# Retention attention in front of a feed-forward block: four 64x64 tiles of TensorE, two sequences loaded head by head, the state summed in SBUF

## Chip, cores and metric

One core of one Trainium2 chip. The metric is the device time of one execution in microseconds (us); lower is better. The kernel before takes 219.63 us (median of four runs, 219.4 to 220.01; the prediction was made from the first three, median 219.77). Engines: PE is TensorE's matmul, PEld its weight load, DVE is VectorE, ACT is ScalarE, POOL is GpSimd, SP the queue that issues stores and transposes.

## The reference

A decayed linear attention over 4 sequences of 768 positions with 8 heads of 64, then a feed-forward block with a sine activation. Its output is 3072 x 512 in float32.

```python
# q, k, v: (4, 8, 768, 64)
for t in range(S):
    state = gamma * state + outer(k[t], v[t])        # 64 x 64 per head
    y[t] = (1 / sqrt(64)) * q[t] @ state
x = y as (3072, 512)
h = x @ w_in                                         # (3072, 2048)
s = sin(alpha * h)
out = (h + s * s / (alpha + 1e-9)) @ w_out           # (3072, 512)
```

## The kernel before

Each sequence is cut into six chunks of 128 positions, so there are 24 chunks, taken in the order "first chunk of each sequence, then the rest of sequence 0, 1, 2, 3". The decay is divided out beforehand, so that the state becomes a plain running sum. Per chunk there are four kinds of small matmul, together called a burst here: scores (k against q), old state times q, masked scores times v (the mix), and the sum of k times v that is added to the state.

```python
def stage_S(j):                    # the state's sum lives in PSUM over the whole sequence
    if c == 0:
        st["ps"] = psum.tile([128, NP, D], F32, name="ps", tag="ps")
    ...matmul(ps[64 * e:64 * e + 64, p, :], k of the head, v of the head,
              start=(c == 0 and p == 0), ...)
def keep_S(j, ps):                 # two copies of 64x256 on ScalarE, straight from PSUM
    nc.scalar.copy(s_bd[(j % NCH + 1) % 2][r, :, r], ps[r, :, :])
def stage_M(j):
    py = psum.tile([128, NP, 128], F32, name="py", tag="ty")
    ...old state, mix...
    ps = stage_S(j)
    nc.vector.tensor_mul(x, py, qg[:, c])            # xT
    keep_S(j, ps)
```

The feed-forward work is cut into slots. A slot is one 128-wide block of hidden units: four products into a PSUM tile `ph`, then sine and square on ScalarE, then on VectorE the sum `gT`, which also frees `ph`. Output matmuls into `po` fill TensorE between slots.

```python
class Slot:
    self.ph = psum.tile([128, nf, w], F32, name="ph", tag=tag, bufs=4 if tag == "mm" else 1)
    ...4 matmuls; nc.scalar.activation(out=self.s, in_=self.ph, func=Sin)
    def sq(self, eng):  # "A": Square on ScalarE, "D": s * s on VectorE
    def add(self):      # VectorE: gT = s * rec_alpha + ph
def ff_out(g, ts, f):
    if (g, ts) not in po:
        po[g, ts] = psum.tile([128, d_model], F32, name="po", tag="mm", bufs=4)
```

Count the PSUM in units of one 128x512 float32 tile. The scores tile `pa` has two units, `ps` one, `ty` one, the ring `mm` four: eight. While the first four chunks pass through the feed-forward block, two output accumulators are held open for some 20 us. `ps` and `ty` are free at that time, and the schedule puts them there:

```python
    po[0, 0] = psum.tile([128, d_model], F32, name="po", tag="ps")
    po[0, 1] = psum.tile([128, d_model], F32, name="po", tag="ty")
    F((0,), range(4))              # output matmuls that fill TensorE between slots
```

Of the kernel before, what the change touches and what calls it, by code (L numbers as in the profile page):

```python
# [15 lines left out]
def kernel(  # L16
# [9 lines left out]
):  # L26

# [45 lines left out]
    def load_chunk(j, names="qkv"):  # L73
        for name, src in (("q", q), ("k", k), ("v", v)):
            if name not in names:
                continue
            if name == "v":
                t = big.tile([128, H, D], BF16, name="vr", tag="vr", bufs=NJ)
            else:
                if ("qk", j) not in raw:  # L80
                    raw["qk", j] = big.tile([128, 2, H, D], BF16, name="qkr", tag="qkr", bufs=NJ)
                t = raw["qk", j][:, "qk".index(name)]
            nc.gpsimd.dma_start(out=t, in_=chunk_of(src, j))  # L83
            raw[name, j] = t

# [4 lines left out]
    def load_w_in(i):  # L90
        nc.gpsimd.dma_start(out=w_in[:, :, i * fw:(i + 1) * fw], in_=w_in_v[:, :, i * fw:(i + 1) * fw])
# [6 lines left out]
    for name, src in (("q", q), ("k", k)):  # L98
        near[name] = big.tile([128, H, D], F32, name=f"{name}0")
        nc.sync.dma_start(out=near[name], in_=chunk_of(src, 0))  # L100
        raw[name, 0] = big.tile([128, H, D], BF16, name=f"{name}b")
# [9 lines left out]
    def scale_v(j, eng):  # L111
        eng.tensor_mul(raw["v", j], raw["v", j], kg[:, j % NCH, :, None].to_broadcast([128, H, D]))  # L112
# [38 lines left out]
    for p in range(NP):  # L151
        for e in range(2):
            nc.vector.memset(lgp[64 * e:64 * e + 64, p:p + 1], lng[2 * p + e])
# [3 lines left out]
                         lg[:, None, :].to_broadcast([128, NCH, H]))  # L157
    qg = consts.tile([128, NCH, NP, C], F32, name="qg")
# [12 lines left out]
    s_bd = [big.tile([128, NP, 128], BF16, name=f"s_bd{i}") for i in range(2)]  # L171
# [3 lines left out]
    xT = {}  # L175

    def half_T(j, i, eng):
# [4 lines left out]
        for p in range(NP):  # L182
            nc.tensor.transpose(pt[:, p, :], raw["qk"[i], j][:, 2 * p:2 * p + 2, :].rearrange("p h d -> p (h d)"), ident)
# [6 lines left out]
    def stage_T(j, eng=None, tag="ty"):  # L190
        pt = psum.tile([128, 2 * NP, 128], BF16, name="pt", tag=tag, bufs=4 if tag == "mm" else 1)
        st["qkT", j] = work.tile([128, 2 * NP, 128], BF16, name="qkT", tag="qkT", bufs=6)
        for i in range(2):
            for p in range(NP):
                nc.tensor.transpose(pt[:, i * NP + p, :],
                                    raw["qk"[i], j][:, 2 * p:2 * p + 2, :].rearrange("p h d -> p (h d)"), ident)
# [5 lines left out]
    def turn(j):  # L202

        st["qkT", j] = work.tile([128, 2 * NP, 128], BF16, name="qkT", tag="qkT", bufs=6)
        nc.sync.dma_start_transpose(out=st["qkT", j], in_=raw["qk", j].rearrange("p i h d -> p (i h d)"))

    def stage_A(j):
        qkT = st["qkT", j]
        pa = psum.tile([128, 2, NP, 128], F32, name="pa", tag="pa")
        for p in range(NP):  # L210
            for e in range(2):
                r = slice(64 * e, 64 * e + 64)
                nc.tensor.matmul(pa[:, e, p, :], qkT[r, NP + p, :], qkT[r, p, :],  # L213
                                 start=(p == 0), stop=True, skip_group_check=True)
        aT = work.tile([128, 2, NP, 128], BF16, name="aT", tag="aT", bufs=2)
        m = dec.rearrange("p e n t -> p (e n) t") if j % NCH == 0 else mask_bc
        nc.vector.tensor_mul(aT.rearrange("p e n t -> p (e n) t"), pa.rearrange("p e n t -> p (e n) t"), m)  # L217
        st["aT", j] = aT

    def stage_S(j):  # L220
        c = j % NCH
        if c == 0:
            st["ps"] = psum.tile([128, NP, D], F32, name="ps", tag="ps")
        ps = st["ps"]
        for p in range(NP):
            for e in range(2):
                nc.tensor.matmul(ps[64 * e:64 * e + 64, p, :], raw["k", j][:, 2 * p + e, :], raw["v", j][:, 2 * p + e, :],  # L227
                                 start=(c == 0 and p == 0), stop=True, skip_group_check=True)
        return ps

    def keep_S(j, ps):
        for e in range(2):
            r = slice(64 * e, 64 * e + 64)
            nc.scalar.copy(s_bd[(j % NCH + 1) % 2][r, :, r], ps[r, :, :])  # L234

    def stage_M(j):
        c = j % NCH
# [3 lines left out]
        qkT, aT, vs = st["qkT", j], st["aT", j], raw["v", j]  # L241
        py = psum.tile([128, NP, 128], F32, name="py", tag="ty")
        if c > 0:
            for p in range(NP):
                for e in range(2):
                    r = slice(64 * e, 64 * e + 64)
                    nc.tensor.matmul(py[r, p, :], s_bd[c % 2][:, p, r], qkT[:, p, :],  # L247
                                     start=(p == 0), stop=True, skip_group_check=True)
        for p in range(NP):
            for e in range(2):  # L250
                nc.tensor.matmul(py[64 * e:64 * e + 64, p, :], vs[:, 2 * p + e, :], aT[:, e, p, :],  # L251
                                 start=(c == 0 and p == 0), stop=True, skip_group_check=True)
        x = xT[g][:, :, i * C:(i + 1) * C]
        if c == 0:
            nc.scalar.copy(x, py)
            return
        ps = stage_S(j) if c < NCH - 1 else None
        nc.vector.tensor_mul(x, py, qg[:, c])  # L258
        if ps is not None:
            keep_S(j, ps)  # L260
# [4 lines left out]
    class Slot:  # L265


        def __init__(self, g, f, cols=None, nf=1, tag="mm"):
# [7 lines left out]
            self.s = work.tile([128, nf, w], F32, name="s", tag="s", bufs=5)  # L276
            for m, f in enumerate(self.fs):
                for i in range(KS):
                    nc.tensor.matmul(self.ph[:, m, :], w_in[:, i, f * 128:(f + 1) * 128], xT[g][:, i, self.lo:self.hi],  # L279
                                     start=(m == 0 and i == 0), stop=(i == KS - 1), skip_group_check=True)  # L280
# [18 lines left out]
    end = (NG - 1, sizes[-1] - 1)  # L299

    def ff_out(g, ts, f):
# [4 lines left out]
        if f == FF - 1:  # L306
            take(g, ts)

    def take(g, ts):
        o_sb = work.tile([128, d_model], F32, name="o_sb", tag="o_sb", bufs=3)  # L310
        if (g, ts) == end:
            h = d_model // 2
            nc.vector.tensor_copy(o_sb[:, :h], po[g, ts][:, :h])
            nc.scalar.copy(o_sb[:, h:], po[g, ts][:, h:])
        else:
            nc.scalar.copy(o_sb, po[g, ts])  # L316
        nc.sync.dma_start(out=out_view[:, groups[g][ts], :], in_=o_sb)
# [5 lines left out]
    pal = psum.tile([128, FF], F32, name="pal", tag="ps")  # L323
# [22 lines left out]
    stage_A(e0)  # L346
# [3 lines left out]
    half_T(e1, 1, nc.vector)  # L350
    nc.tensor.transpose(pal, alpha_row, ident_f)
    stage_M(e0)
    grow(1)
    idle_work(1)
    stage_A(e1)
# [5 lines left out]
    stage_M(e1)  # L361
    grow(3)
    nc.scalar.copy(alpha_sb, pal)
    nc.scalar.activation(out=tiny, in_=warm[:, 0:1], func=ACTF.Sin)
    stage_A(e2)
# [4 lines left out]
    stage_M(e2)  # L370
# [22 lines left out]
    def A(j):  # L393
        return lambda: stage_A(j)

    def M(j):
        return lambda: stage_M(j)

    def SK(j):
        return lambda: keep_S(j, stage_S(j))  # L400
# [16 lines left out]
    for t in s_bd:  # L417
        nc.vector.memset(t, 0.0)
    b = early(1)
    a.sq("A").add()  # L420
    a = early(2)
    b.sq("A")
    c = early(3)
    a.sq("A")
    stage_T(e3)
    b.add()
    b = early(4, "ps")
    c.sq("A")
# [3 lines left out]
    stage_A(e3)  # L432
    c.add()
    c = early(6)
    a.sq("A")
    b.add()
    b = early(7)
    c.sq("A")
    stage_M(e3)
# [3 lines left out]
    po[0, 0] = psum.tile([128, d_model], F32, name="po", tag="ps")  # L443
    po[0, 1] = psum.tile([128, d_model], F32, name="po", tag="ty")
# [6 lines left out]
    a = Slot(0, 8)  # L451
    b = Slot(0, 4, (n3, n4), 4)
    a.sq("A").add()
    a = Slot(0, 9)
    b.sq("D").add()
    F((0, 1), (4,))
    b = Slot(0, 10)
    a.sq("A").add()
    F((0, 1), (5,))
    a = Slot(0, 11)  # L460
    b.sq("D").add()
    decay_table(4)
    F((0, 1), (6, 7))
    b = Slot(0, 12)
    a.sq("A").add()
    decay_table(5)
    F((0, 1), (8,))
    a = Slot(0, 13)
# [96 lines left out]
```

## Time and profile before

| | before |
|---|---|
| time, median of four | 219.63 us |
| span of the profiled run | 217.5 us |
| TensorE busy | 203.8 us, 94% |
| ScalarE, VectorE, GpSimd busy | 162.8, 128.1, 90.1 us |
| mean granted TensorE clock | 0.999 |

I cut the span into four stages at marks: the first product; the first 256-column product (the stage of chunks 5 and 6); the next 512-column stage (chunks 7 to 10); and the first output group of the 512-column stage after that. Rows of busy time by stretch give the stretch, its length, then busy us (and instructions) of PE, PEld, DVE, ACT and POOL, the granted clock, the share of the transfer engines and GB/s.

### The profile page before, as it was taken

The numbers are of one execution on the slowest core, as the hardware profiler recorded it, in microseconds if no ns is written. First come the engines' busy times: TensorE is split into PE (matmuls) and PEld (weight loads), VectorE is DVE, ScalarE is ACT, GpSimd is POOL, SyncE is SP. The second block draws the span as 40 slices with busy tenths as digits, with TensorE's granted clock in tenths as the row PEclk, the third lists the DMA queues.
The fourth block names the chain that finished last, engine by engine and source line by source line (L and its number), as shares of the span: only waits on it lengthen the run. The fifth ranks groups of instructions, "written<-read, shape, count | busy, mean of one in ns | idle before, by whom it ended". The sixth has DMA issues, their size and how long they took to land.

```text
span 217.5 us, 4218 instructions
## 1 busy us (share of the span) xinstructions
PE 203.8 (94%) x1634; PEld 107.5 (49%) x1661; DVE 128.1 (59%) x213; ACT 162.8 (75%) x311; POOL 90.1 (41%) x105
## 2 busy tenths in 40 slices
PE   7798899999989999999999999999999999999992
PEld 3444554467764545445455445454544544555540
DVE  4686659867895767766466566366464555233310
ACT  7678796658889999789768768777868876766610
POOL 8975335999889885896981000000000000000000
PEclk9999999999999999999999999999999999999999
DMA  9999999999999999999999146237011101111121
GB/s 132 151 193 191 205 207 164 154 207 161 164 151 182 163 120 154 112 160 175 135 188 107 23 96 77 60 60 96 7 47 51 48 0 51 48 48 48 51 94 50
DMA packets 99508, 24.67 MB, mean 113 GB/s; under 512 B 92304, under 2 KB 96416, under 8 KB 99488
## 3 DMA queue, kind: packets, MB, share of 16 engines
q0 software_dynamic: 77024, 13.37, 84.0%
q1 hardware_dynamic: 22464, 11.02, 26.4%
q8 instruction: 13, 0.21, 0.4%
q14 instruction: 7, 0.06, 0.1%
HBM read 27.27 MB, written 6.29 MB: 154 GB/s over the span
## 4 chain that ended last, share of the span: by engine, by line
PE 74%; DVE 9%; DMA 4%; POOL 4%; ACT 4%; issue 3%; POOLq 0%; ACTq 0%
PE po L304 35%; PE ph L279 31%; DMA qkr<-in_k_dram 4%; DVE gT L294 4%; PE py L247 3%; PE pa L213 2%; POOL qkr L83 2%; ACT s L282 2%; DVE aT L217 2%; PE py L251 2%; POOL vr L83 1%; DVE xT L258 1%; PE ps L227 1%; DVE s L289 1%; ACT s L287 1%
## 5 line engine op out<-in xcount | busy, mean ns | idle before, releaser
L294 DVE SCALAR_TENSOR_TENSOR gT<-s,rec_alpha,ph 128x512 bf16<-128x512 f32 (+3 forms) x120 | 74.1, 637 | 68.1 <-ACT s L287 67.5
L279 PE MATMUL ph<-xT,w_in 128*128 128x512 bf16 (+3 forms) x478 | 97.9, 336 | 1.1 <-DVE gT L294 0.6
L304 PE MATMUL po<-w_out,gT 128*128 128x512 bf16 x360 | 94.1, 379 | 3.8 <-issue 2.9
L282 ACT ACTIVATE s<-ph,alpha_sb 128x512 f32<-128x512 f32 (+3 forms) x120 | 69.6, 601 | 34.0 <-PE ph L279 33.9
L279 PEld LDWEIGHTS <-w_in 128*128 128x128 bf16 x480 | 45.5, 98 | 42.6 <-issue 2.1
L287 ACT ACTIVATE s<-s 128x512 f32<-128x512 f32 (+1 forms) x94 | 58.4, 621 | 2.6
L304 PEld LDWEIGHTS <-gT 128*128 128x128 bf16 x384 | 35.2, 98 | 38.2 <-issue 0.6
L112 POOL TENSOR_TENSOR vr<-vr,kg 128x512 bf16<-128x512 bf16 x21 | 22.0, 1056 | 12.2 <-DMA vr<-in_v_dram 12.2
L217 DVE TENSOR_TENSOR aT<-pa,mask 128x1024 bf16<-128x1024 f32 x20 | 24.4, 1220 | 0.3 <-PE pa L213 0.3
L83 POOL DMA_DIRECT2D vr<-in_v_dram x24 | 21.7, 904 | 3.0 <-DMA w_in<-in_moe_w_in_dram 1.7
L83 POOL DMA_DIRECT2D qkr<-in_q_dram x23 | 21.3, 925 | 4.0 <-DMA w_out<-in_moe_w_out_dram 1.6
L83 POOL DMA_DIRECT2D qkr<-in_k_dram x23 | 20.4, 887 | 3.8 <-DMA w_out<-in_moe_w_out_dram 3.3
L234 ACT CAST s_bd<-ps 64x256 bf16<-64x256 f32 x40 | 14.4, 360 | 2.4 <-PE ps L227 2.1
L316 ACT COPY o_sb<-po 128x512 f32<-128x512 f32 x23 | 13.1, 576 | 3.9 <-PE po L304 3.9
L258 DVE TENSOR_TENSOR xT<-py,qg 128x512 bf16<-128x512 f32 x20 | 13.7, 684 | 2.6 <-PE py L251 2.5
L328 PE MATMUL spare<-warm 128*128 128x512 bf16 x27 | 9.3, 465 | 1.4 <-DVE warm L131 1.2
L213 PEld LDWEIGHTS <-qkT 64*128 64x128 bf16 x192 | 5.4, 94 | 9.3 <-issue 7.1
L251 PE MATMUL py<-aT,vr 128*64 128x128 bf16 x192 | 9.5, 220 | 0.4 <-DVE rec_alpha L366 0.2
L213 PE MATMUL pa<-qkT 64*128 64x128 bf16 x192 | 9.5, 219 | 0.4 <-ACT qkT L186 0.2
L247 PE MATMUL py<-qkT,s_bd 128*64 128x128 bf16 x160 | 8.3, 224 | 0.7 <-DVE xT L258 0.7
L247 PEld LDWEIGHTS <-s_bd 128*64 128x64 bf16 x160 | 5.4, 109 | 4.8 <-issue 2.0
L251 PEld LDWEIGHTS <-vr 128*64 128x64 bf16 x192 | 6.9, 110 | 1.3 <-issue 1.0
(59 smaller groups left out, 68.8 us busy)
## 6 DMA issues: line engine op xcount, KB each, us to landing
out_dram<-o_sb SPq DMA_DIRECT2D x24, 256.0 KB, 2.3
vr<-in_v_dram POOLq DMA_DIRECT2D x24, 128.0 KB, 6.2
qkr<-in_q_dram POOLq DMA_DIRECT2D x23, 128.0 KB, 5.6
qkr<-in_k_dram POOLq DMA_DIRECT2D x23, 128.0 KB, 5.8
w_in<-in_moe_w_in_dram POOLq DMA_DIRECT2D x4, 512.0 KB, 11.1
w_out<-in_moe_w_out_dram POOLq DMA_DIRECT2D x4, 512.0 KB, 14.8
q<-in_q_dram SPq DMA_DIRECT2D x1, 256.0 KB, 3.4
k<-in_k_dram SPq DMA_DIRECT2D x1, 256.0 KB, 4.7
```

What stands on the lines that cost most here:

```text
L83: nc.gpsimd.dma_start(out=t, in_=chunk_of(src, j))
L112: eng.tensor_mul(raw["v", j], raw["v", j], kg[:, j % NCH, :, None].to_broadcast([128, H, D]))
L213: nc.tensor.matmul(pa[:, e, p, :], qkT[r, NP + p, :], qkT[r, p, :], start=(p == 0), stop=True, skip_group_check=True)
L217: nc.vector.tensor_mul(aT.rearrange("p e n t -> p (e n) t"), pa.rearrange("p e n t -> p (e n) t"), m)
L247: nc.tensor.matmul(py[r, p, :], s_bd[c % 2][:, p, r], qkT[:, p, :], start=(p == 0), stop=True, skip_group_check=True)
L251: nc.tensor.matmul(py[64 * e:64 * e + 64, p, :], vs[:, 2 * p + e, :], aT[:, e, p, :], start=(c == 0 and p == 0), stop=True, skip_group_che ...
L258: nc.vector.tensor_mul(x, py, qg[:, c])
L279: nc.tensor.matmul(self.ph[:, m, :], w_in[:, i, f * 128:(f + 1) * 128], xT[g][:, i, self.lo:self.hi], start=(m == 0 and i == 0), stop=(i = ...
L282: nc.scalar.activation(out=self.s[:, m, :], in_=self.ph[:, m, :], func=ACTF.Sin, scale=alpha_sb[:, f:f + 1])
L287: nc.scalar.activation(out=self.s, in_=self.s, func=ACTF.Square)
L294: nc.vector.scalar_tensor_tensor(gT[self.g][:, f, self.lo:self.hi], self.s[:, m, :], rec_alpha[:, f:f + 1], self.ph[:, m, :], op0=ALU.mult ...
L304: nc.tensor.matmul(po[g, ts], gT[g][:, f, ts * C:(ts + 1) * C], w_out[:, f, :], start=(f == 0), stop=(f == FF - 1))
```

## The change

The intent is to spend less TensorE time on attention, by three means, and a little at the end:

- Small matmuls are cut into 64x64 pieces, so that four of them lie on TensorE at once: old state and scores for sequences 0 and 1, scores, mix and sums for sequences 2 and 3. (Mix and sums of 0 and 1 keep their 128x64 tiles; the old state of 2 and 3 becomes four full 128x128 matmuls.)
- Sequences 2 and 3 are loaded head by head with 64 positions on each half of the partitions (`load_seq`), so that the block of scores that the mask makes zero is never computed (768 columns in place of 1024).
- The state is summed on VectorE in SBUF (`s_f`); the product of one chunk no longer lives in PSUM.
- The last output tile is stored in pieces of 256, 128 and 128 columns.

The diff, cut to its core:

```diff
-    def stage_S(j):
-        if c == 0:
-            st["ps"] = psum.tile([128, NP, D], F32, name="ps", tag="ps")
-    def keep_S(j, ps):
-            nc.scalar.copy(s_bd[(j % NCH + 1) % 2][r, :, r], ps[r, :, :])
+    def new_py(j):
+        st["py", j] = psum.tile([128, 2, 512], F32, name="py", tag="py")   # state sums in here too
+    def keep(j, py):
+        new = py[:, :, 256:384].rearrange("p b (m d) -> p m b d", m=2)
+        nc.vector.tensor_add(s_f, s_f, new)          # tensor_copy at the first chunk
+        nc.scalar.copy(s[half(0), :, 0:4:3], s_f[half(0)])
+        nc.scalar.copy(s[half(1), :, 1:3], s_f[half(1)])
+    def mix(j, first=None):
+        ...sums(now, py)
+        nc.vector.tensor_mul(x_of(j), py[:, :, 0:256]..., qg[:, c]...)
+        keep(now, py)
+    def burst(old, new, first=None):
+        inter(old)        # old state
+        scores(new)       # scores of the next chunk, and VectorE's masked product aT
+        mix(old, first)
...
-    po[0, 0] = psum.tile([128, d_model], F32, name="po", tag="ps")
-    po[0, 1] = psum.tile([128, d_model], F32, name="po", tag="ty")
...
-    a = Slot(0, 8)
+    a = Slot(0, 8, nf=2, tag="py")
...
-    a = Slot(0, 11)
-    b.sq("D").add()
+    b = Slot(0, 11)
+    a.sq("D").add()
     decay_table(4)
...
+    load_seq(2)
+    load_seq(3)
...
+    last_tile(NG - 1, sizes[-1] - 1)
```

`py` now has two units, and `ps` and `ty` are gone: pa 2, py 2, mm 4, again eight. Two pairs of slots of the first stage (8 and 9, 12 and 13) take `py` instead, and some squares move from ScalarE to VectorE. VectorE also scales 19 of the v tiles, in place of 3 (GpSimd did the others), and the slots around the fourth first chunk come in another order.

## The prediction

> **What bounds the kernel now.** I read the page first (busy shares, then the chain that ended last), then the TensorE timeline of one burst of attention, then the busy time by stage, then the GpSimd timeline, which shows when loads land. From the page:
>
> ```profile
> PE 203.8 (94%) x1634; PEld 107.5 (49%) x1661; DVE 128.1 (59%) x213; ACT 162.8 (75%) x311; POOL 90.1 (41%) x105
> ...
> DMA  9999999999999999999999146237011101111121
> ...
> PE 74%; DVE 9%; DMA 4%; POOL 4%; ACT 4%; issue 3%; POOLq 0%; ACTq 0%
> PE po L304 35%; PE ph L279 31%; DMA qkr<-in_k_dram 4%; DVE gT L294 4%; PE py L247 3%; PE pa L213 2%; POOL qkr L83 2%; ACT s L282 2%; DVE aT L217 2%; PE py L251 2%; POOL vr L83 1%; DVE xT L258 1%; PE ps L227 1%; DVE s L289 1%; ACT s L287 1%
> ```
>
> The chain is TensorE, and two thirds of the span are the two feed-forward products (L279, L304), which the change leaves as they are. The DMA row matters too: the engines are full for the first 22 of 40 slices, some 119 us, because the loads last that long. Busy time by stage, one row per stretch of time, with each engine's busy us:
>
> ```profile
> 89.00:121.50 32.50, 31.87 (x270) 15.87 (x270) 19.50 (x26) 25.69 (x47) 22.82 (x25) 1.00 1.71 142
> 121.50:153.70 32.20, 31.67 (x253) 15.56 (x256) 18.65 (x25) 25.04 (x45) 0.00 (x0) 1.00 0.39 67
> 153.70:185.70 32.00, 31.58 (x192) 14.87 (x195) 16.16 (x22) 24.75 (x43) 0.00 (x0) 1.00 0.09 34
> ```
>
> TensorE is busy 98% of these; VectorE 58% and ScalarE 78% (19 and 25 of 32 us) have room. So here a microsecond of TensorE saved is a microsecond of time, as long as nothing makes TensorE wait. One slot and one burst, from the TensorE timeline (start, duration, line, count):
>
> ```profile
> 100.26 1.03 PE L279 MATMUL ph<-xT,w_in 128*128 128x512 bf16 x4
> 101.22 0.40 PE L213 MATMUL pa<-qkT 64*128 64x128 bf16 x8
> 101.55 0.41 PE L247 MATMUL py<-qkT,s_bd 128*64 128x128 bf16 x8
> 101.79 0.39 PE L251 MATMUL py<-aT,vr 128*64 128x128 bf16 x8
> 102.02 0.29 PE L227 MATMUL ps<-vr,qkr 128*64 128x64 bf16 x8
> 102.47 0.81 PE L304 MATMUL po<-w_out,gT 128*128 128x512 bf16 x3 [0.16 <-issue]
> ```
>
> Four 512-column matmuls take 0.863 us from start to start elsewhere (103.11 to 103.97), so the burst starts at 101.12. Its end is 102.25, not 102.47: the next group should have four matmuls and shows three, so one record is missing and the "issue" wait is not real. The burst costs 1.13 us. This is confirmed by the period: bursts begin at 101.22 and 109.25, 8.03 us apart, and 32 matmuls at 0.216 us are 6.90.
>
> **What the Trainium skill says.** "TensorEngine Tiling (Array Packing)", Key Properties: a change of tiling mode drains TensorE. The trace agrees: from the last product to the scores 0.96 us pass in place of 0.863, so 0.10 a switch; scores to the next group (64x128 to 128x64) is 0.33, while L247 to L251, the same mode, is 0.24. The same page, Tiling Modes: 64x64 gives four independent tiles; no run here shows four yet. "TensorE: Matmul & The Clock Gate", Wait — 56ns, not 53.3ns?: starts never come closer than about 25 ns. Here the measurement decides: eight matmuls of 64 columns span 0.29 us with 0.196 each (the mean of their row), so they start (0.29 - 0.196)/7 = 13 ns apart. The 128-column scores start (0.40 - 0.219)/7 = 26 ns apart. So two tiles do share the time, down to 13 ns at least. "DMA: Bandwidth & Descriptors", Queues, rings and completion order: each engine takes its queue rows in turn, so a transpose on the SP queue shares with loads that are queued. That fits transposes that land in 3.1 to 8.9 us, median 6.0, while the loads run.
>
> **The change, part by part.** In 128 columns one tile needs 53 ns (0.216/4); with four at once that is 13.4 ns a matmul, a rate that the trace has shown. 64 columns at four tiles would be 6.7 ns, which it has not; I take 6.7 to 13.4.
>
> *Sequences 0 and 1, ten chunks.* Old state: 8 matmuls, now 4 tiles, 0.107 us (was 0.21). Scores: 16 halves at 13.4, 0.214 (as before). Mix and sums are as before, 0.214 + 0.107. Three switches, 0.30, as before. Sum 0.94, with the 0.03 that two groups lose now (0.24 and 0.23 against 0.214): 0.97. It saves 0.16, times ten: 1.6 us.
>
> *Sequences 2 and 3, ten chunks.* Old state: four full matmuls of 128 columns, 0.225 with overhead, in the mode of the products, so without a switch. Scores and mix: 8 of 128 and 8 of 64 columns each, 0.16 to 0.21 each. Sums: 16 of 64, 0.11 to 0.21. Two switches, 0.20. Sum 0.86 to 1.06, against 1.13: it saves 0.07 to 0.27, say 0.17, times ten: 1.7 us. The masked block saves little matmul time; it takes a quarter off the 1.22 us score product of VectorE (768 in place of 1024 columns, about 0.28 us by the step from 512 columns, 0.68, to 1024, 1.22), which is not the bound.
>
> *VectorE.* Added: the state sum of 256 columns, about 0.42 (a 256-column copy out of PSUM is 0.423), some 20 times; scaling of v, 0.74 each, some twelve moved here from GpSimd. Per stage of four chunks that is 4 x (0.42 + 0.74 - 0.27) = 3.6 us on 19: 22 of 31. Hidden on average. After a burst the product of the slot comes later by 0.42 - 0.28 = 0.14; the four PSUM buffers leave some 2.4 us (a slot's product ends at 104.15; the third slot after it starts at 106.6). Costs nothing.
>
> *The start.* The products begin at 15.49. VectorE gets eight small operations (about 0.15 to 0.2 each, as the 0.16 and 0.21 rows) before the third score product, where it had 0.50 us idle: some 0.7 us later. GpSimd issues four more loads ahead of the fourth first chunk, 0.7 us each, but its k waited 9.4 us in a full queue, so it lands about as before; its transposes, which TensorE waited for twice (0.43 and 0.45), come one slot later in the program. I set these off against each other: 0.
>
> *The end.* The last product ends at 213.4, the span at 217.5: two half copies in turn (0.42, then 0.37), then the store. In pieces of 256, 128 and 128 columns, the last copy is about 0.28 and its store smaller, so 0.7 less; shorter matmuls (57 ns against 53) cost 0.1. Net gain 0.6.
>
> Sum of the parts: 1.6 + 1.7 + 0.6 = 3.9 us less, 215.9, if nothing waits.
>
> **The rivals.** *First, the late sequence.* Chunk 13 (the first of sequence 2) now needs all 16 loads of q and k of its sequence, not its own two. From the GpSimd timeline, scaling waits show when a v lands: chunk order 6, 10 and 13 land at 43.9, 57.86 and 71.48.
>
> ```profile
> 57.86 1.04 POOL L112 TENSOR_TENSOR vr<-vr,kg 128x512 bf16<-128x512 bf16 x1 [0.88 <-DMA vr<-in_v_dram]
> ...
> 71.48 1.04 POOL L112 TENSOR_TENSOR vr<-vr,kg 128x512 bf16<-128x512 bf16 x1 [0.96 <-DMA vr<-in_v_dram]
> ...
> 87.58 1.04 POOL L112 TENSOR_TENSOR vr<-vr,kg 128x512 bf16<-128x512 bf16 x1 [2.94 <-DMA vr<-in_v_dram]
> ```
>
> That is 3.5 us a chunk with few transposes, 4.5 with one each. After 70 to 71 come ten of fifteen parts of five chunks, 3.33 chunks: 11.7 us at 3.5, and some 1.5 for stores and two transposes. So q and k land near 84, and the transpose 3 to 6 us later, 87 to 90. TensorE wants it at slot 14 of the stage that begins at 65 now (near 64 after): 14 x 1.30 + 0.86 + 3 bursts, near 86. A wait of 1 to 4 us in the in-order queue, which adds in full. Against it: GpSimd no longer waits for each v, so it issues ahead, and by 84 the loads may have been faster than I take them; loads into 64 partitions each are of the same 256-byte rows, and nothing shows whether they go faster or slower. I give a wait above 1 us a bit over half, so 1.8 on average. It would make 217 to 220.
>
> *Second, four tiles do not overlap*, or the sequencer needs 16 ns for a load and a matmul. Then scores, mix and sums of a wide chunk are 3 x 16 x 16 ns = 0.77, the burst 1.19, and ten cost 0.6 more; the others gain about 0.9. Near 219. For it: 13 ns is the fastest seen. Against: two tiles scaled as they should.
>
> *Third, VectorE or ScalarE becomes the bound* where the stages shrink: ScalarE 25 of 31 us is the closest. Less likely; it would give back some of the gain, 217 to 218.
>
> **Range and chances.** 219.8 - 3.9 + 1.8 is 217.7; I say 217.5. Without the wait and at the best tile rate it is about 214.5, with a long wait and no overlap 222; so 213.8 to 221.5. Faster by over 2% needs under 215.4: no wait and all of the gain, 0.23. Slower needs 224.2, two rivals at once: 0.06. The rest is 0.71.
>
> **What would show it.** In the changed profile: bursts of 0.95 to 1.05 us between products in the later stages; starts of 64x64 matmuls 13 ns apart or less; VectorE near 140 us busy; the wait of TensorE for the transposed tile near 86 us, named after a DMA or a score group; first product near 15.5 to 16.5; tail near 3.4 us. I am wrong if a burst stays at 1.13, if the loads of the late sequences come well before 80, or if the early stage (15 to 48 us), where I set gains against losses, moved by over 2 us.

## More of the kernel before

```profile
15.49:48.21 32.72, 29.82 (x252) 16.13 (x256) 24.77 (x43) 23.62 (x49) 19.68 (x23) 1.00 1.82 187
48.21:65.09 16.88, 15.62 (x222) 12.02 (x224) 14.05 (x25) 14.38 (x33) 15.40 (x18) 1.00 2.00 161
65.09:91.81 26.72, 25.83 (x218) 12.80 (x220) 18.50 (x25) 23.51 (x42) 21.58 (x24) 1.00 1.93 148
```

In the second and third stage ScalarE is busy 14.38 of 16.88 and 23.51 of 26.72 us, that is 85% and 88%, and in the second VectorE has 83%. These two stages have far less room than the 78% and 58% of the later ones.

## The result, and the profile after

The changed kernel takes 241.75 us (median of four runs, 240.59 to 242.81) against 219.63. The ratio is 1.1004, with a 95% interval of 1.095 to 1.1058: 10% slower. Ratios here are the mean time of one kernel's fast runs over that of the other's fast runs of the same rounds, so not quite the quotient of the medians. The output is correct, as it is in all runs below.

From the page of the changed kernel (the profiled execution is the slowest of the four, 242.81 us): busy time, the tenths of TensorE and its clock in 40 slices, and the chain that ended last.

```profile
PE 214.6 (89%) x1949; PEld 111.5 (46%) x1949; DVE 145.9 (61%) x262; ACT 163.4 (68%) x308; POOL 86.0 (36%) x115
...
PE   8977939478995898888799999999999999999994
...
PEclk9999986959999779999999999999999999999999
...
PE 68%; DVE 15%; ACT 13%; issue 2%; DVEq 0%; ACTq 0%
```

TensorE's share of the chain went from 74% to 68% and that of VectorE and ScalarE from 9% and 4% to 15% and 13%. The clock row falls below 9 three times in the first 15 slices (some 90 us); before, it was 9 everywhere (mean 0.999, now 0.958). The late slices are as full as ever. The stages say how much:

```profile
16.05:62.43 46.38, 34.96 (x273) 17.68 (x272) 27.39 (x45) 21.91 (x44) 37.66 (x45) 0.85 1.90 171
62.43:84.82 22.39, 17.95 (x266) 12.28 (x265) 15.41 (x30) 15.71 (x34) 15.72 (x23) 0.92 2.06 154
84.82:116.64 31.82, 28.28 (x261) 13.02 (x261) 23.97 (x37) 23.04 (x41) 18.06 (x26) 0.95 1.42 122
116.64:238.00 121.36, 120.27 (x1053) 62.00 (x1051) 67.27 (x105) 90.86 (x160) 0.00 (x0) 1.00 0.22 59
```

| stage | before | after | more | of it TensorE idle | of it TensorE busy longer |
|---|---|---|---|---|---|
| until the first product | 15.49 | 16.05 | +0.56 | | |
| first stage | 32.72 | 46.38 | +13.66 | +8.5 | +5.1 |
| 256-column stage | 16.88 | 22.39 | +5.51 | +3.2 | +2.3 |
| 512-column stage | 26.72 | 31.82 | +5.10 | +2.7 | +2.5 |
| the rest of the span | 125.7 | 124.4 | -1.3 | | |

Idle is the length less the busy time of the row; "busy longer" is mostly the lower clock. So the loss of 23.5 us of span lies wholly before 117 us, in stages for which the prediction expected none (0 for the start, and a gain of 1.6 us by the bursts of sequences 0 and 1). The late part did become shorter, by 1.3 us.

What the bursts became, from TensorE's timeline, for a chunk of sequence 2 or 3 (start, duration, line, count):

```profile
120.47 1.03 PE L424 MATMUL ph<-xT,w_in 128*128 128x512 bf16 x4
121.33 0.39 PE L339 MATMUL py<-qkT,s_b 128*128 128x128 bf16 x4
121.65 0.25 PE L364 MATMUL pa<-qkT 64*64 64x128 bf16 x4
...
122.02 0.30 PE L314 MATMUL py<-v_seq,qk_seq 64*64 64x64 bf16 x16
122.25 1.04 PE L448 MATMUL po<-w_out,gT 128*128 128x512 bf16 x4
```

From 121.33 to 122.25 are 0.92 us, against 1.13 before. The old state follows the products without the 0.10 of a change of mode. Sixteen 64x64 matmuls of 64 columns span 0.30 us at 0.193 each (the mean of their row), so they start (0.30 - 0.193)/15 = 7 ns apart: four tiles do overlap. A burst of sequence 0 or 1 (89.95 to 90.98 in the same timeline) takes 1.03. The tail, from the end of the last matmul to the end of the span, is 3.0 us against 4.1. The idea of the change works.

What went wrong stands in the waits of TensorE (who waited for whom: us in all, times, longest). Before, TensorE's waits for `gT` were 0.6 us for the products, and its longest list entry for a state or `xT` was 0.7.

```profile
PE ph L424 <- DVE gT L439: 5.8, 4, 3.9
PE pt L254 <- DVE gT L439: 4.4, 1, 4.4
PE py L344 <- ACT s_b L324: 3.3, 2, 2.5
```

The first two are waits for a PSUM buffer: `gT` is VectorE's last reading of a `ph`. They lie in the first stage. On the timelines of TensorE, of VectorE just before the wait's end, and of ScalarE:

```profile
30.89 0.59 PE L448 MATMUL po<-w_out,gT 128*128 128x512 bf16 x2
35.40 1.86 PE L424 MATMUL ph<-xT,w_in 128*128 128x512 bf16 x4 [3.92 <-DVE gT L439]
37.06 1.91 PE L448 MATMUL po<-w_out,gT 128*128 128x512 bf16 x4
...
49.71 1.01 PE L254 MATMUL pt<-ident,qkr 128*128 128x128 bf16 x8 [4.43 <-DVE gT L439]
```

```profile
33.50 0.69 DVE L434 TENSOR_TENSOR s<-s 128x512 f32<-128x512 f32 x1
34.22 1.12 DVE L439 SCALAR_TENSOR_TENSOR gT<-s,rec_alpha,ph 128x128 bf16<-128x128 f32 x4
```

```profile
37.30 0.69 ACT L427 ACTIVATE s<-ph,alpha_sb 128x512 f32<-128x512 f32 x1 [4.58 <-PE ph L424]
```

TensorE has stopped at 31.5 and may write the next `ph` only when the four small `gT` at 34.22 have ended. In turn ScalarE waits 4.58 us for that `ph`. And after the wait the four products take 1.66 us from start to start (35.40 to 37.06) in place of 0.863. The Trainium skill has a rule for this second cost: "TensorE: Matmul & The Clock Gate", Part 1, says that the array's clock falls to half after an idle window of about 3.4 us and comes back after a busy one of that length. This trace agrees for the waits of 3.92 and 4.43 us. But it has the half clock after shorter waits too, of 2.51 us (shown further below; eight products of 256 columns then take 1.87 us and not 1.04) and of 1.51 us:

```profile
79.85 1.87 PE L424 MATMUL ph<-xT,w_in 128*128 128x256 bf16 x8
84.82 1.76 PE L424 MATMUL ph<-xT,w_in 128*128 128x512 bf16 x4 [1.51 <-DVE xT L394]
```

The third wait, for `s_b`, is of another kind. ScalarE's own waits in the changed kernel, and then the group of the copies in the kernel before for comparison (busy, mean ns, then idle before and what ended it):

```profile
ACT s_b L324 <- DVE s_f L322: 22.5, 16, 2.5
ACT s_b L324 <- DVE s_f L320: 6.8, 4, 2.9
```

```profile
L234 ACT CAST s_bd<-ps 64x256 bf16<-64x256 f32 x40 | 14.4, 360 | 2.4 <-PE ps L227 2.1
```

ScalarE stands still for 29.3 us in front of the copies of the state; before it was 2.1. Of these, 7.1 and 7.6 us lie in the 256-column and the 512-column stage, where it had no room, 4.6 in the first stage and 10.1 in the late part, which lost nothing against the kernel before. One such place on VectorE's, ScalarE's and TensorE's timelines:

```profile
74.69 1.22 DVE L358 TENSOR_TENSOR aT<-pa,mask 128x1024 bf16<-128x1024 f32 x1
75.83 0.68 DVE L394 TENSOR_TENSOR xT<-py,qg 128x512 bf16<-128x512 f32 x1
76.43 0.41 DVE L322 TENSOR_TENSOR s_f<-s_f,py 128x256 f32<-128x256 f32 x1
```

```profile
76.87 0.41 ACT L324 CAST s_b<-s_f 64x256 bf16<-64x256 f32 x1 [1.61 <-DVE s_f L322]
```

```profile
77.33 0.24 PE L344 MATMUL py<-qkT,s_b 64*64 64x128 bf16 x1 [2.51 <-ACT s_b L324]
```

The sum `s_f` is third in VectorE's queue, behind the masked product of the *next* chunk and `xT`. The copy on ScalarE stands in line for it, and every sine and square behind the copy stands too.

### The profile page after: what moved, and what is told of

Same layout as the page of the kernel before. It is cut to its first block, busy times and chain, and to the rows that moved or that the text cites. A ratio compares the mean times of both kernels' runs of the same rounds, so it can differ in the third digit from the quotient of the medians.

```text
span 241.0 us, 4826 instructions
## 1 busy us (share of the span) xinstructions
PE 214.6 (89%) x1949; PEld 111.5 (46%) x1949; DVE 145.9 (61%) x262; ACT 163.4 (68%) x308; POOL 86.0 (36%) x115
## 4 chain that ended last, share of the span: by engine, by line
PE 68%; DVE 15%; ACT 13%; issue 2%; DVEq 0%; ACTq 0%
PE po L448 30%; PE ph L424 27%; ACT s L427 6%; DVE gT L439 5%; ACT s L432 4%; PE spare L480 3%; DVE aT L358 3%; DVE xT L394 2%; DVE aT L280 1%; PE poh L463 1%; DVE s L434 1%; ACT s_b L324 1%; ACT s_b L325 1%; PE py L339 1%; PE pa L364 1%
## 5 line engine op out<-in xcount | busy, mean ns | idle before, releaser
L324 ACT CAST s_b<-s_f 64x256 bf16<-64x256 f32 x20 | 8.1, 405 | 29.4 <-DVE s_f L322 22.5
L358 DVE TENSOR_TENSOR aT<-pa,mask 128x1024 bf16<-128x1024 f32 x10 | 12.2, 1220 | 4.6 <-PE pa L355 4.6
L89 POOL DMA_DIRECT2D vr<-in_v_dram x14 | 12.7, 910 | 1.8 <-DMA w_out<-in_moe_w_out_dram 1.0
L104 POOL DMA_DIRECT2D qk_seq<-in_k_dram x16 | 11.4, 729 | 5.5 <-DMA qk_seq<-in_q_dram 5.5
L89 POOL DMA_DIRECT2D qkr<-in_q_dram x13 | 12.0, 922 | 1.6 <-DMA w_out<-in_moe_w_out_dram 0.9
L89 POOL DMA_DIRECT2D qkr<-in_k_dram x13 | 11.7, 902 | 2.1 <-DMA w_out<-in_moe_w_out_dram 2.0
L104 POOL DMA_DIRECT2D v_seq<-in_v_dram x16 | 11.5, 773 | 2.3 <-DMA qk_seq<-in_k_dram 2.1
L104 POOL DMA_DIRECT2D qk_seq<-in_q_dram x16 | 11.6, 771 | 0.3
L372 DVE TENSOR_TENSOR aT<-pa,maskq 128x768 bf16<-128x768 f32 x10 | 9.6, 957 | 1.0
L325 ACT CAST s_b<-s_f 64x256 bf16<-64x256 f32 x20 | 8.0, 401 | 0.4
L142 DVE TENSOR_TENSOR v_seq<-v_seq,kgq 128x512 bf16<-128x512 bf16 x10 | 6.8, 684 | 0.0
```

What stands on the lines that cost most here:

```text
L89: nc.gpsimd.dma_start(out=t, in_=chunk_of(src, j))
L104: nc.gpsimd.dma_start(out=o, in_=src[bt, h, C:, :].rearrange("(f i) d -> i f d", i=64))
L324: nc.scalar.copy(s[half(0), :, 0:4:3], s_f[half(0)])
L358: nc.vector.tensor_mul(aT.rearrange("p e n t -> p (e n) t"), pa.rearrange("p e n t -> p (e n) t"), mask_bc)
```

## The experiments

So there are two suspects. **Theory A**: the two accumulators now take half of the ring of four in the first stage, from some 26 us on; the products starve for `ph`, and the halved clock doubles the damage. **Theory C**: in the next two stages, the state's sum on VectorE holds up ScalarE's in-order queue. Rivals: the squares moved to VectorE (first stage), the halved clock alone, the amount of work on ScalarE or VectorE rather than its order, and the late load of sequence 2. In the texts below, Theory B is the first of these rivals (VectorE, with the squares, is the bound of the first stage), and Theory D is that TensorE waits because VectorE is late, whatever ScalarE does.

Experiments with one run each are of unknown state. The kernel before, run beside them, took 219.0, 218.79 and 219.58 us on the three chips; the changed kernel's four runs lie 2.2 us apart. I therefore read single runs from their stage marks and take no total that differs by less than some 2 us as a result.

### 1. The first stage: squares, buffers, clock

*e1_squares*: the squares of the first stage back on ScalarE.

```diff
-    a.sq("D").add()          # slot 10, and the same for slots 12 to 15
+    a.sq("A").add()
```

> The changed kernel with one thing undone: in the first stage (four early chunks, about 24 to 62 us) the squares of slots 10 and 12 to 15 go back from VectorE to ScalarE; the PSUM buffers stay as changed. Theory A (two PSUM buffers of the ring of four are held by the two output accumulators, so TensorE has only two for its first products): the first wait of TensorE, 3.9 us near 35 us, stays; the second, 4.4 us near 49 us, shrinks by a part; in all at most 5 us less, about 237 to 240. Theory B (VectorE does the squares in a row and is the bound of the stage): both waits go, about 230.

*e2_banks*: the accumulators get the two units of `py`, which is free in this stage; the paired slots become single slots of the ring, and the first state sum, which needs `py`, starts later.

```diff
+    pp = psum.tile([128, 2, 512], F32, name="po", tag="py")
+    po[0, 0], po[0, 1] = pp[:, 0, :], pp[:, 1, :]
-    a = Slot(0, 8, nf=2, tag="py")
+    a = Slot(0, 8)
+    c = Slot(0, 9)
...
-    begin(e0)                # now after the next three output matmuls
```

> The changed kernel with the output accumulators of the first stage put into the two banks of the attention output (idle at that time), so that all four buffers of the ring are for the first products, which become eight slots of 512 columns; the first state sum moves behind the stage, as it needs those banks. The squares stay on the engines that the change gave them. Theory A: both waits go or fall below 1 us each, TensorE stays at full clock until 60 us, the stage ends some 10 us or more earlier, about 228 to 232. Theory B: the waits stay, within 3 us of 241.8.

*e3_banks_squares*: e2 with the order of slots and squares of the kernel before (A and D in turn).

> Both undone: the accumulators out of the ring, and the squares and slots in the order and on the engines of the kernel before. Theory A: within 2 us of the run with the banks alone. Theory B: much faster than either. Both: the first slot of 256 columns begins at 48 to 50 us, as in the kernel before (48.2) and not at 62.4; about 226 to 229, as the 5.5 us lost in the next stage and some 5 us in the one after are not touched, but some of that was the low clock after waits, which should go as well.

*e4_filler*: the changed kernel with 12 matmuls of no use before each of the two long waits, into the free `pa`. They keep TensorE busy, so the wait stays but the clock should not fall.

```diff
+    warmup(12)               # 12 matmuls of 512 columns, 2.6 us
     b = Slot(0, 11)
...
+    warmup(12)
     stage_T(P[4], nc.scalar)
```

> The changed kernel with 12 idle matmuls of 512 columns (2.6 us of work whose result nobody reads) in each of the two long waits of TensorE of the first stage, so that no gap is longer than some 2 us. If the halved clock after each wait costs time of its own, the granted clock stays at 1.0 until 60 us and the time falls by 2 to 4 us although TensorE has 5.2 us more to do; if the clock is only a symptom, the time stays or rises.

| | time | first stage | mean clock |
|---|---|---|---|
| changed | 241.75 | 46.4 | 0.958 |
| e1, squares | 240.09 | 44.0 | 0.964 |
| e2, buffers | 235.55 | 40.2 | 0.985 |
| e3, both | 231.15 | 36.5 | 0.993 |
| e4, fillers | 239.55 | 43.2 | 0.986 |
| before | 219.0 | 32.7 (its profile above) | 1.000 |

The buffers alone give 6.2 us, the order of slots and squares on top of them another 4.4; the squares alone give 1.7, which is within the spread, but 2.4 in their stage. The waits for `gT` tell the two theories apart: in e1 the one of 3.9 us stays and the one of 4.4 falls to 2.1, as Theory A had it; in e2 the longest is 1.0 us, and the clock stays full until 50 us. Yet e2 came out above the 228 to 232 us that were expected. In their stage the parts are 2.4 and 6.2 us alone and 9.9 together, so nearly a sum: the order and the squares have a share of their own. The fillers show what the clock was worth. The wait for `gT` is cut to 1.32 us, and the products after it run at full speed:

```profile
36.75 1.02 PE L424 MATMUL ph<-xT,w_in 128*128 128x512 bf16 x4 [1.32 <-DVE gT L439]
```

The stage shrinks by 3.2 us although TensorE does 24 x 0.216 = 5.2 us of useless work. The halved clock was thus a good part of the damage, but giving back the buffers and the order of the squares (e3) gains three times as much.

### 2. The copies of the state

All three stand on e3. *e5_copies_on_vector* takes the copies off ScalarE:

```diff
-        nc.scalar.copy(s[half(0), :, 0:4:3], s_f[half(0)])
+        nc.vector.tensor_copy(s[half(0), :, 0:4:3], s_f[half(0)])
```

> On top of the run with banks and squares undone (231.15 us): the two copies of the summed state to bf16 go from ScalarE to VectorE, right behind the sum. Theory C (in the two stages after the first, ScalarE has no room: 0.69 + 0.63 us of sine and square for each slot of 1.30, and each copy of the state makes it wait some 1.6 us for the sum that VectorE does behind two larger products): ScalarE no longer waits, the stage of 256-column slots shrinks from 22.2 us to about 18 and the next from 29.2 to about 27, as VectorE, with 0.8 us more a chunk, comes near its own bound; about 225. Theory D (TensorE waits for PSUM buffers because VectorE is late, not ScalarE): these stages grow, 232 or more.

*e6_copies_later* keeps them on ScalarE but puts them behind the sine and square of the next slot, so that the sum is there when their turn comes:

```diff
-        nc.scalar.copy(s[half(0), ...], s_f[half(0)])
+        pending.append(lambda: nc.scalar.copy(s[half(0), ...], s_f[half(0)]))
...
             now = Slot(g, n * nf, nf=nf).sq("A")
+            flush()
```

> On the same base (231.15 us): the two copies of the state stay on ScalarE but stand in its queue behind the sine and square of the next slot, by when the sum is done; where the next burst needs the state at once they go just before it. Nothing else. Theory C: ScalarE's waits for the sum (22.5 us in all in the changed kernel) fall to a few us; the stage of 512-column slots shrinks from 29.2 us to about 25; the one of 256-column slots, with bursts in three slots running, gains little or loses, as the state then comes too late. About 226 to 227. Theory D: unchanged within 1 us.

*e7_state_first* leaves all work where it is and changes only VectorE's order after a burst: sum, `xT`, masked product, in place of masked product, `xT`, sum.

```diff
         if now is not None:
             sums(now, py)
-        nc.vector.tensor_mul(x_of(j), ...)
         if now is not None:
             keep(now, py)
+        nc.vector.tensor_mul(x_of(j), ...)
...
         inter(old)
-        scores(new)
+        masked = scores(new, late=True)
         mix(old, first)
+        masked()
```

> On the same base (231.15 us): in each burst VectorE does the state sum first, then the scaled output, then the masked scores of the next chunk (before: masked scores, scaled output, state sum). No instruction is added, taken away or moved to another engine. Theory C: ScalarE waits less than 0.5 us a chunk, the two stages fall to about 18 and 25 us, 222 to 224 in all. Theory D: unchanged within 1 us, as the work of VectorE is the same.

| | time | 256-column stage | 512-column stage |
|---|---|---|---|
| e3 | 231.15 | 22.2 | 30.2 |
| e5, copies on VectorE | 232.03 | 22.2 | 29.9 |
| e6, copies later | 232.69 | 23.2 | 29.2 |
| e7, sum first | 223.81 | 18.5 | 26.6 |
| before | 218.79 | 16.9 | 26.7 |

e5 and e6 gain nothing in all, and they are the instructive misses. Both take the wait from ScalarE (from 27.9 us in e3 to none and to 3.7). But TensorE needs the copy for the old state of the next burst. Its waits for the first of the two copies in e5 and in e6, over the whole run (3.3 in e3):

```profile
PE py L344 <- DVE s_b L324: 4.2, 3, 2.3
```

```profile
PE py L352 <- ACT s_b L331: 5.2, 4, 1.9
```

In the 256-column stage e6 has 4.4 us of this, e3 2.5 and e5 1.7. In the 512-column stage none of the three has any. There VectorE, which now copies as well, is busy 27.67 of 29.88 us in e5; e6 begins the stage at half clock, after two waits of 1.9 us, and its first two slots take 4.1 us in place of some 2.6, so that without this it would be near 27.7 (an estimate from these rows): there moving the copy did help. (The first stages, 39.8 and 41.1 us, are 3 to 5 longer than e3's. In e5, 3.5 us of waits for the two copies lie in it, 1.2 in e3; e6 waits 1.6 us for loads and 1.0 for a scaled v.)

So moving the copy is not enough; what brings both stages back is that the sum *is ready earlier*. e7 has the same instructions on the same engines as e3, and gains 7.3 us: 3.7 and 3.5 in the two stages and 2.3 in the rest, less 2.3 in the first. That refutes Theory D as it was stated. One thing is not separated: with the masked product last, `xT` too is ready earlier. In e7 the 512-column stage is as long as that of the kernel before:

```profile
73.33:99.97 26.64, 25.40 (x256) 12.59 (x260) 23.66 (x36) 24.18 (x42) 22.25 (x32) 1.00 1.99 161
```

ScalarE's waits for the sum fell from 27.9 us in e3 to 6.9 + 1.7 = 8.6, with none in the 512-column stage. In e7 something else came to light. TensorE waited once 3.1 us for VectorE's scaling of a v, on VectorE's and GpSimd's timelines:

```profile
50.48 2.60 DVE L142 TENSOR_TENSOR vr<-vr,kg 128x512 bf16<-128x512 bf16 x1
```

```profile
50.45 2.08 POOL L142 TENSOR_TENSOR vr<-vr,kg 128x512 bf16<-128x512 bf16 x2
```

The same instruction took 0.69 us elsewhere in that trace. The Trainium skill, "SBUF — State Buffer", Who interferes with whom, says that a VectorE instruction with two SBUF inputs contends with a GpSimd instruction that reads SBUF, and that whoever comes second is blocked. The numbers fit: VectorE comes 0.03 us after GpSimd and ends 0.55 us after the second of its two products.

### 3. The same in reverse, on the kernel before

*e10_before_ring*: the kernel before without the two lines that place the accumulators. They come from the ring then; `ps` and `ty` stay idle.

```diff
-    po[0, 0] = psum.tile([128, d_model], F32, name="po", tag="ps")
-    po[0, 1] = psum.tile([128, d_model], F32, name="po", tag="ty")
```

> The other way round: the kernel before with two lines taken out, so that its two first output accumulators come from the ring of four that the first products use, as in the change. Nothing else. Theory A (two buffers left for the products): TensorE waits for VectorE's products in the first stage, the 256-column stage begins 4 to 9 us later than 48.2 us, the total is 223 to 228. If the buffers do nothing by themselves, 219 as before.

*e11_before_state_sbuf*: the kernel before with the state summed in SBUF and nothing else (`s_f` lies in a tile that is free by then).

```diff
-        if c == 0:
-            st["ps"] = psum.tile([128, NP, D], F32, name="ps", tag="ps")
+        ps = psum.tile([128, NP, D], F32, name="ps", tag="ps")       # start at each chunk
...
+        nc.vector.tensor_add(s_f, s_f, ps)
-            nc.scalar.copy(s_bd[(j % NCH + 1) % 2][r, :, r], ps[r, :, :])
+            nc.scalar.copy(s_bd[(j % NCH + 1) % 2][r, :, r], s_f[r, :, :])
```

> The kernel before with the state summed in SBUF by VectorE, as the change does, behind the scaled output; the matmuls, their tiles and all else as before. Theory C: ScalarE waits 1 to 1.6 us a chunk for the sum, the stage of 256-column slots takes 20 to 22 us and not 16.9, the first of 512-column slots 28 and not 26.7 to the same mark; 224 to 228 in all. If the copies find room, 219 to 220.

| | time | first stage | 256-column | 512-column | rest |
|---|---|---|---|---|---|
| before (same chip) | 219.58 | 32.7 | 16.9 | 26.7 | 125.7 |
| e10, accumulators in the ring | 234.66 | 48.1 | 16.9 | 26.7 | 125.7 |
| e11, state in SBUF | 232.88 | 35.9 | 20.5 | 32.3 | 127.1 |

(The stages of the row "before" are those of its profile above.) Both runs lost more than was expected (223 to 228 and 224 to 228 us). Two lines cost 15.1 us, all of it in the first stage. The waits of TensorE in e10, and the one at the same place of its timeline:

```profile
PE ph L279 <- DVE gT L294: 10.2, 6, 2.5
```

```profile
33.01 1.87 PE L279 MATMUL ph<-xT,w_in 128*128 128x512 bf16 x4 [2.53 <-DVE gT L294]
```

Here the clock was already halved after a wait of 2.53 us. Before it lie a wait of 1.97 us and 1.05 us of work, so it was not one unbroken idle window; why it was enough, these runs don't settle. The state in SBUF costs 13.3 us, 9.3 of it in the two tight stages. Each cause by itself brings back the loss of its own stages: A the first (+15.4 there against +13.7 in the changed kernel), C the next two (+3.7 and +5.6 against +5.5 and +5.1). Together 28.4 us are more than the 22.1 that were lost, so they do not simply add. Of e11's 3.2 us in the first stage, 1.2 are lost before its first state sum, where TensorE waits 1.6 us for a load, and 2.0 after it; and in the last part the changed kernel gains 1.3 where e11 loses 1.4.

### 4. Can the change be made to pay?

*e8_together* puts the accumulators into `pa` instead of `py`, and takes the sum first and the tables early.

> The whole put together: accumulators of the first stage in the banks of the scores (so that they wait for nothing), squares as in the kernel before, the state sum first, and the eight small tables of VectorE moved into its idle time near 4 us. If the two theories (buffers in the first stage, ScalarE waiting for the state in the next two) are the cause of the loss, this gets below the kernel before: about 217 to 219, with the first slot of 256 columns at 48 to 49 us, against 222 if something else is missing. A wait for the late sequence 2 near 85 us, which the slower kernels hid, could show here, 1 to 4 us.

It took 224.84 us, no better than e7: its first stage is 40.0 us. The second accumulator's last matmul had to wait 2.19 us for the copy of the first, because both lie in one tile.

*e9_best* is e7 with what e7 and e8 had shown: both last matmuls of the pair before either copy, the v scaled early, the tables early, and two output matmuls held back to fill the gap before the 512-column stage.

```diff
-    F((0, 1), (15,))
+    for t in range(2):
+        ff_out(0, t, 15, take_now=False)
+    take(0, 0)
+    take(0, 1)
```

> The run with banks, squares and the state sum first (223.81 us), with four more waits taken away: the eight small tables in idle time near 4 us; the last matmuls of both accumulators of the first stage before either copy (they share one tile, so the second waited 1.37 us for the copy of the first); the scaling of v of the second attention chunk moved ahead of the burst (behind it, it took 2.60 us beside a product on GpSimd, in place of 0.68, and TensorE waited 3.1 us); two output matmuls kept back to fill the wait of 1.65 us before the stage of 512-column slots. If these are what is left of the loss: stage of 256-column slots begins near 50 us (before 48.2, changed 62.4), 217 to 219.5.

It took 221.45 us against 219.58 of the kernel before on the same chip. Its stages are 36.8, 19.2 and 26.6, its rest 122.1: the late part now gains 3.6 us against the kernel before, and the first two stages still lose 4.0 and 2.3.

*e13_tuned* is e9 with one compact copy of the state for sequences 0 and 1, one transpose behind the accumulators' copies, and the mask's table in the first stage, timed in five rounds.

```diff
+        if j // NCH < 2:
+            nc.scalar.copy(s_c[(j % NCH + 1) % 2], s_f)
+            return
```

> From the run with all repairs (221.45 us, begins of stages 51.75, 70.96, mark 97.6), four more: the transposes of the second attention chunk moved behind the copies of the first accumulators (TensorE waited 1.0 us for those); the state of sequences 0 and 1 copied in one instruction of 256 columns and not two of half the partitions (their 64x64 tiles need no zero blocks); the last mask built in idle time of VectorE in the first stage, 1 us, and not ahead of the stage of 512-column slots. If the rest of the loss against the kernel before is order and ScalarE, 217.5 to 219; if the two middle stages are bound by VectorE, which has 0.41 us of state sum a chunk and one product more there, they stay near 19 and 26.6 us and the total at 220 to 221.

It took 222.27 us, ratio 1.0157 with an interval of 1.0124 to 1.019 (before: 219.38). The first stage is 35.0, but the second 20.7: TensorE waits there once 2.1 us for a `qkT` that a transfer brings (not the transpose that was moved). The scores behind this wait begin at 65.12 us, those of e9 at 65.23 after a wait of 1.27, so what was gained before is lost there.

So with both causes repaired the change still does not pay; e13 is between 1 and 2% slower, which is within the 2% that count as the same here. e8, e9 and e13 came out 5.8, 2.0 and 1.3 us above the upper ends of what was expected.

*e12_before_last_tile* goes the other way: the kernel before with only the stores of the last tile in three pieces.

```diff
-    for fn in out_pieces(NG - 1, range(sizes[-1])):
+    for fn in out_pieces(NG - 1, range(sizes[-1] - 1)):
         fn()
+    last_tile(NG - 1, sizes[-1] - 1)
```

> The kernel before with the last output tile in pieces of 256, 128 and 128 columns, as the change has it. By the estimate of the prediction 0.6 us less than the kernel before of the same chip; the tail from the last matmul to the end 3.4 us and not 4.1.

It took 218.52 us against 219.58. One run can't carry 0.5%, so *e14_before_last_tile_timed* is the same kernel in five rounds.

> The same kernel as the one with only the last output tile in pieces, timed in five rounds: 0.4 to 0.6 per cent less than the kernel before, the interval clear of 1.

Its median is 218.81 us, ratio 0.9969 with an interval of 0.9944 to 0.9995. (Its profiled execution, with a clock of 0.661, is left out.) On the profile of e12, the last copy comes at 213.76 and the span ends at 216.7. This is the only version that beats both kernels: 0.3%, less than the 0.4 to 0.6 expected, a small gain that five rounds just separate from nothing.

## Why the prediction was wrong

The prediction was 217.5 us with a range of 213.8 to 221.5, and gave "slower by over 2%" a chance of 0.06. It came 24 us above. By its own steps:

1. **The bursts.** Right in mechanism and near in size. Sequences 0 and 1: 1.03 us where 0.97 was worked out. Sequences 2 and 3: 0.92, inside the 0.86 to 1.06. The fine rate of 6.7 to 13.4 ns was left open; it is 7. The two rows of the sum were 1.6 and 1.7 us; measured bursts would give 10 x 0.10 = 1.0 and 10 x 0.21 = 2.1. (A slip that changes nothing: at the best tile rate and without a wait its parts give 214.9, not 214.5.)
2. **Where that gain is earned.** "So here a microsecond of TensorE saved is a microsecond of time" holds for the late stages only. The ten bursts of sequences 0 and 1 lie before the late stages, where the waits on VectorE and ScalarE come; even e9 gains nothing to speak of there (26.64 us in the 512-column stage against 26.72). In the changed kernel the late part, too, gives only 1.3 us: each chunk carries a delay of some 0.12 us (its period is 7.96, in e9 7.84), and TensorE waits once 1.09 us for the copy of an output tile. In e9 both are gone and the late part gains 3.6, where ten bursts and the tail are 2.1 + 1.1 = 3.2.
3. **"The four PSUM buffers leave some 2.4 us ... Costs nothing."** This step failed. The count of four is read in the late stages. In the first stage two of the four were now taken by the accumulators; the diff shows it in the two lines that it removes, and the prediction didn't ask where their contents go. e10 measures those two lines: 15.1 us.
4. **"The start ... I set these off against each other: 0."** It looked at loads, tables and transposes up to 15 us, and that was right: the first product came at 16.05 (said: 15.5 to 16.5). But the first stage itself, 15 to 48 us, was never worked through. It lost 13.7 us. The last sentence of the prediction named this stage as the place where it could be wrong.
5. **"VectorE ... Hidden on average."** Its busy time is 145.9 us (said: near 140): 17.8 us were added and not some 12, with sixteen scalings of v moved in place of twelve. But e7 shows that the amount was not the point. This step failed too. The sum has a consumer, ScalarE's copy, in a queue that takes its instructions in turn; the delay of VectorE's order, not its load, was handed on. e5 and e6, which move the copy, gain nothing in all; e7, which moves the sum (and `xT`) ahead, gains 7.3 us; e11, the sum in SBUF alone, costs 13.3.
6. **The third rival**, VectorE or ScalarE as the bound, is the one that came nearest, but was given 217 to 218 us because "25 of 31 us is the closest" was taken from the stages between 89 and 186 us. Between 48 and 92 us, ScalarE's share was 85 to 88%, and no part of the prediction reads those rows.
7. **The first rival**, the late load of sequence 2, got most of the attention, and a place in the sum (1.8 us). No run has a wait of TensorE for it, but it is hidden rather than refuted: everywhere TensorE comes later than the 86 us of the prediction. In e9 the first transpose of sequence 2 starts at 88.15, after a wait of 1.9 us for a load of k, and lands 5.9 us later, near 94.05 (87 to 90 was worked out); TensorE first uses it at 94.15. A kernel that kept the pace of the prediction would probably have had to wait; no run shows it. **The second rival**, no overlap of four tiles, is refuted by the 7 ns.
8. **The end.** Right: the tail is 1.1 us shorter where 0.7 was worked out, and the time fell by 0.3% in e14, some 0.7 us, near the net 0.6. (The 1.06 us of e12 are a single run.)

What stays open: in e9 the first two stages are 4.0 and 2.3 us longer than before, although buffers and order are repaired. The trace places the 4.0: 1.5 us are lost by 27.5 us, around the fourth first chunk, where e9 waits 0.78 us for a `qkT` and 0.56 for a masked product and the kernel before does not; the other 2.5 come after 43 us, with waits of 1.00 us for the copy of an accumulator in `py`, 0.56 for a masked product and 0.41 for `xT`. No run undoes these one by one. In the 256-column stage the profile puts TensorE's waits in e9 all down to VectorE (1.5 us for `xT`, 1.3 for `gT`, 0.6 for a masked product), but the 1.3 stands before the scores that in e13 wait for a transfer until 65.12 us, so it may be that transfer too; VectorE is busy 15.59 us where it was 14.05, with four state sums of 0.41 that the kernel before does not have. That these sums make the 2.3 us is argued, not shown.

## What to carry to other kernels

When a change takes a buffer away or merges two, list for every stage who else was living in it, because a tile that is free in one stage is often what another stage rests on; two lines were worth 15 us of 220 here. When a result moves to an engine with room to spare, look at its place in that engine's queue and at who stands in line for it, not at the busy share. And read the shares of *each* stage, above all of the stages that the profile's averages hide: the gain was computed where TensorE is the bound and lost where it is not.

## What the Trainium skill lacked or had wrong

- "TensorE: Matmul & The Clock Gate", Wait — 56ns, not 53.3ns?, gives a floor of about 25 ns between the starts of matmuls, however small. With two tiles at once the kernel before starts them 13 ns apart, and with four tiles of 64x64 and 64 columns the changed kernel does it in 7 ns: (0.30 - 0.193)/15. So the floor does not hold across tiles. The sentence does not say so, though the page's later part on packing has closer starts for matmuls on different tiles.
- The same page's rule on the clock gate fits the long waits (1.66 us in place of 0.863 for four products after a wait of 3.92 us), but its abstract rule, no idle gaps of more than about 3.4 us, is not enough: in the changed kernel the clock was halved after waits of 2.51 and 1.51 us too, and in e10 after 1.97 and 2.53 us with 1.05 us of work between them. The page mentions clocks that swing through short idle times, but gives no length for them.
- No page that I found says what long-lived accumulators in a ring of PSUM buffers can cost: two of four held through one stage cost 15.1 us (e10).
- Nor does one say what a result can cost that is ready late for the in-order queue of another engine: 29.3 us of standing still on ScalarE, and 7.3 us of time by the order of three instructions on VectorE (e3 against e7).
